# A two-layer decode block streaming 1.08 GB: chunk pairs in 32 KB rows at both ends of the stream, one memory for ring, weights and kept V, and V one slot further behind K

## The chip, the cores and the metric

The kernel runs on one core of one Trainium2 chip. The metric is the device time of one launch in microseconds (us), median of several runs. Engines are named as in the profile: PE (TensorE matmul), PEld (its weight load), DVE (VectorE), ACT (ScalarE), POOL (GpSimd) and SP (SyncE, which issues nearly all DMAs here).

## The reference, cut to what matters

```python
# x: (2, 1, 512); k_cache, v_cache: (2, 8, 32768, 128); wq: (512, 4096); wo: (4096, 512), all float32
x = x + A(layernorm(x))      # grouped-query attention over the cache
x = x + B(layernorm(x))      # token-mixing MLP, F = 1792
x = x + A(layernorm(x))      # the same caches and weights again
x = x + B(layernorm(x))
# A: q = x @ wq, 32 query heads, 4 of them share one of 8 K/V heads
#    p = softmax(q k^T / sqrt(128)); o = p v; return o @ wo
# B: y = w2 . gelu(w1 * layernorm(x) + b1) + b2, per channel
```

The caches of one layer are 537 MB and do not fit on the chip, so both layers read them from memory: about 1.08 GB in one launch.

## The kernel before, in words

The work is cut into 32 **units**: 2 layers x 2 batch rows x 8 K/V heads. A unit's K and its V are cut into 8 **chunks** each of 2 MB (128 partitions, rows of `CK` = 4096 floats, 16 KB). In main memory a chunk is one contiguous block, so a row of 16 KB is followed at once by the next partition's row.

One hand-written loop over **slots** `s` sets the whole order (lines 553 to 563): in slot `s` the kernel loads and uses K chunk `s` (counted over all units), then V chunk `s - 8 - LAG`. So V runs one unit and `LAG` = 1 slot behind K. Two tables, `pre` and `post`, hang the small steps onto slots: `make_q` (the query for the next unit, L171), `max_1`, `max_2` and the exponentials (L219 to L235), `denominators` (L300), `out_1` and `out_2` (L315 to L331), and the mixer of a finished layer row.

`k_chunk` (L183) takes a tile of the pool `ring`, issues the load on SP (L187), and runs 8 matmuls of 512 columns (L196; 16 in the trace, since a float32 matmul is two passes). `v_chunk` (L250) does the same for V (L265, matmuls L275). The pool has `RING` = 3 tiles of 2 MB, shared by K and V: a load can be issued once the matmuls on the chunk three loads earlier are done.

Weights lie in 16 tiles of 1 MB of their own (`wq_sb`, `wo_sb`), each loaded once during the first nine units. For the last head of a layer, part of V (`KEPT`: all of chunk 0, half of chunk 4) stays in the tile `kept` for the second layer, so a few loads are half size or fall away. The very last V chunk is loaded in four pieces (`PIECES`, 16, 8, 4 and 4 of its 32 column groups), so that its matmuls can begin early. After it comes `last_mixer` (L375 on), the closing mixer, whose scratch tiles are two ring tiles; its Gelu runs (L448) are cut where a run would cross from one tile to the other.

The units are ordered so that a layer's mixer runs while other units stream.

Of the kernel before, what the change touches and what calls it, by code (L numbers as in the profile page):

```python
# [8 lines left out]
F32 = mybir.dt.float32  # L9
AF = mybir.ActivationFunctionType  # L10
# [3 lines left out]
P = 128  # L14
CK = 4096
JT = CK // P
NG = 4
SUB = 2
PACK = 4
RING = 3  # L20
LAG = 1
KEPT = {0: 8, 4: 4}
BRIDGE = 3
PIECES = (16, 8, 4, 4)
THIN = 8
QT = 4
GELU_GROUPS = (2, 4, 4, 4)
# [6 lines left out]
def gqa_mixer_kernel(ctx: ExitStack, tc: tile.TileContext, x, kt, v, wq, wo, cols, out):  # L34
# [6 lines left out]

    nc = tc.nc
    B, D = x.shape
    U, NCH, DH, _ = kt.shape
    HKV = U // B
    R = wo.shape[2] // D
    DT = D // P
    FT = (cols.shape[1] - 1) // 3  # L50
    LAYERS = 2
    NU = LAYERS * U
# [3 lines left out]
    assert DH == P and R * PACK * SUB == 32 and PACK * SUB == 2 * QT and DT == NG and R == NG and D == 512  # L56

    const = ctx.enter_context(tc.tile_pool(name="const", bufs=1))
    ring = ctx.enter_context(tc.tile_pool(name="ring", bufs=RING))
    work = ctx.enter_context(tc.tile_pool(name="work", bufs=2))  # L60
    hidden = ctx.enter_context(tc.tile_pool(name="hidden", bufs=1))
    pscore = ctx.enter_context(tc.tile_pool(name="pscore", bufs=2, space=bass.MemoryType.PSUM))
# [6 lines left out]
    nc.vector.memset(xrow, 0.0)  # L69
    for b in range(B):  # L70
        nc.sync.dma_start(xrow[32 * b : 32 * b + 1, :], x[b : b + 1, :])
    wq_sb = [const.tile([P, DT, R * DH], F32, name=f"wq{h}") for h in range(HKV)]
    wo_sb = [const.tile([P, R, D], F32, name=f"wo{h}") for h in range(HKV)]

    def load_wq(h):
        nc.sync.dma_start(wq_sb[h].rearrange("p t c -> p (t c)"), wq[h])

    def load_wo(h):
        nc.sync.dma_start(wo_sb[h].rearrange("p t c -> p (t c)"), wo[h])

    load_wq(0)
    cols_sb = const.tile([P, 3 * FT + 1], F32, name="cols_sb")
# [76 lines left out]
    def unit_of(n):  # L159

        return units[n]
# [18 lines left out]

    sc_ps, S, mx, lsum, oT = {}, {}, {}, {}, {}

    def k_chunk(n, c):  # L183

        layer, b, h = unit_of(n)
        kc = ring.tile([P, CK], F32, name="chunk")
        nc.sync.dma_start(kc, kt[b * HKV + h, c])  # L187
        half, i = divmod(c, PACK)
        if i == 0:
            sc_ps[n] = pscore.tile([P, 512], F32, name="scores")  # L190
        w = CK // (NG * SUB)
        for k in range(SUB):
            at = R * (SUB * i + k)
            q = qpad[n % 2][:, 28 - at : 60 - at]
            for g in range(NG):
                nc.tensor.matmul(  # L196
                    sc_ps[n][32 * g : 32 * g + 32, :],
                    q,
                    kc[:, (k * NG + g) * w : (k * NG + g + 1) * w],
                    start=(i == 0 and k == 0),  # L200
                    stop=(i == PACK - 1 and k == SUB - 1),
                )
        if i == PACK - 1:
            if half == 0:
                S[n] = work.tile([P, HALVES, 512], F32, name="S")
                mx[n] = work.tile([P, HALVES, R], F32, name="mx")
            nc.vector.transpose(S[n][:, half, :], sc_ps[n])  # L207
            nc.vector.tensor_reduce(  # L208
                mx[n][:, half, :],
                S[n][:, half, :].rearrange("p (t h) -> p h t", h=R),  # L210
                axis=AX.X,
                op=ALU.max,
            )
# [27 lines left out]
                accum_out=lsum[n][:, h : h + 1],  # L241
            )

    kept = const.tile([P, sum(KEPT.values()) * QT * DH], F32, name="kept")
    place, at_kept = {}, 0
    for c, quads in KEPT.items():
        place[c] = at_kept
        at_kept += quads * QT * DH

    def v_chunk(n, c):  # L250
        layer, b, h = unit_of(n)
        u = b * HKV + h
        stay = KEPT.get(c, 0) if h == HKV - 1 else 0
        w = QT * DH
        very_last = n == NU - 1 and c == NCH - 1
        if stay:
            own = kept[:, place[c] : place[c] + stay * w]
            if layer == 0:
                nc.sync.dma_start(own, v[u, c, :, : stay * w])
        if stay < JT // QT:  # L260
            vc = ring.tile([P, CK], F32, name="chunk")
            f0 = stay * w
            for k in PIECES if very_last else (JT - stay * QT,):
                part = slice(f0, f0 + k * DH)
                nc.sync.dma_start(vc[:, part], v[u, c, :, part])  # L265
                f0 += k * DH
        half, i = divmod(c, PACK)


        a, c2 = divmod(i, PACK // 2)  # L270
        quads = JT // QT - (THIN // QT if very_last else 0)
        for q in range(quads):
            g = q % NG
            col = (c2 * (JT // QT) + q) * 32 + a * R * QT
            nc.tensor.matmul(  # L275
                acc[32 * g : 32 * g + R * QT, :],
                S[n][:, half, col : col + R * QT],
                (own if q < stay else vc)[:, q * w : (q + 1) * w],
                start=(c == 0 and q < NG),
                stop=(c == NCH - 1 and q >= quads - NG),  # L280
            )

        for j in range(quads * QT, JT):
            q, t = divmod(j, QT)
            g = j % NG
            col = (c2 * (JT // QT) + q) * 32 + a * R * QT + t * R
            nc.tensor.matmul(
                acc[32 * g : 32 * g + R, :DH],
                S[n][:, half, col : col + R],
                vc[:, j * DH : (j + 1) * DH],  # L290
                start=False,
                stop=True,
                skip_group_check=True,
            )
# [80 lines left out]
    def last_mixer(n):  # L375


        layer, b, h = unit_of(n)
        key = (layer, b)
        w = D // 2  # L380
        rw = rows[b]
        y = row_tile()
        p = px[key]
# [14 lines left out]
        for k in range(2):  # L398
            c = slice(k * w, (k + 1) * w)
# [4 lines left out]
        for g in range(NG):  # L404
            c = slice(g * P, (g + 1) * P)
# [4 lines left out]
        deviation(rs, mv)  # L410
        off = work.tile([P, 1], F32, name="off", bufs=1)
        nc.vector.tensor_scalar_mul(off, mv[:, 0:1], -1.0)
        space = [ring.tile([P, CK], F32, name="chunk") for _ in range(2)]
        tiles = [space[k // JT2][:, (k % JT2) * D : (k % JT2 + 1) * D] for k in range(2 * JT2)]
        flat = tiles[2 * JT2 - 1]
        nc.vector.tensor_copy(flat, p)
        scale = work.tile([P, FT], F32, name="scale", bufs=1)
        bias = work.tile([P, FT], F32, name="bias", bufs=1)
# [3 lines left out]
        def project(f):  # L422
            for g in range(NG):
                nc.tensor.matmul(  # L424
                    acc[32 * g : 32 * g + 1, :P],
                    w2c[:, f : f + 1],
                    tiles[f][:, g * P : (g + 1) * P],
                    start=False,
                    stop=(f == FT - 1),
                    skip_group_check=True,  # L430
                )
# [6 lines left out]
        f0 = DIRECT  # L438
        for m in TAIL_GROUPS:
            for f in range(f0, f0 + m):  # L440
                nc.vector.tensor_scalar(
                    tiles[f], flat, scale[:, f : f + 1], bias[:, f : f + 1], op0=ALU.mult, op1=ALU.add
                )

            cut = [f0] + [k for k in (JT2,) if f0 < k < f0 + m] + [f0 + m]
            for lo, hi in zip(cut, cut[1:]):
                u = space[lo // JT2][:, (lo % JT2) * D : ((hi - 1) % JT2 + 1) * D]
                nc.scalar.activation(u, u, AF.Gelu_apprx_tanh)  # L448
            for f in range(f0, f0 + m):
                project(f)  # L450
            f0 += m
        assert f0 == FT
        o = work.tile([P, P], F32, name="o", bufs=1)
# [3 lines left out]
                out[b : b + 1, g * P : (g + 1) * P], o[32 * g : 32 * g + 1, :]  # L457
            )

    JT2 = CK // D  # L460

    hid = {}

# [42 lines left out]
    pre, post = {}, {}  # L506
# [4 lines left out]
    for n in range(NU):  # L511
        layer, b, h = unit_of(n)
# [12 lines left out]
        at(pre, s0 + NCH + 2, denominators, n)  # L525
        e = s0 + 2 * NCH + LAG
        at(pre, e, out_1, n)
# [22 lines left out]
    for r in range(R):  # L550
        make_q(0, r)

    last = max(max(pre), max(post), NU * NCH + NCH + LAG - 1)
    for s in range(last + 1):
        if s < NU * NCH:
            k_chunk(*divmod(s, NCH))
        for f, a in pre.get(s, ()):
            f(*a)
        t = s - NCH - LAG
        if 0 <= t < NU * NCH:  # L560
            v_chunk(*divmod(t, NCH))
        for f, a in post.get(s, ()):
            f(*a)


def _layout(A_x, A_k_cache, A_v_cache, A_wq, A_wo, B_w1, B_b1, B_w2, B_b2):

    import numpy as np

    B, HKV, SK, DH = A_k_cache.shape  # L570
    D = A_x.shape[-1]
    n = SK // CK


    kt = A_k_cache.reshape(B * HKV, n // PACK, 2, PACK // 2, NG, 32, JT // QT, QT // SUB, SUB, DH)
    kt = kt.transpose(0, 1, 2, 7, 9, 8, 4, 3, 6, 5)
    wq = A_wq.reshape(D // P, P, HKV, -1).transpose(2, 1, 0, 3)
    wo = A_wo.reshape(HKV, -1, DH, D).transpose(0, 2, 1, 3)
    cols = [a.reshape(P, -1) for a in (B_w1, B_b1, B_w2)] + [np.broadcast_to(B_b2.reshape(1, 1), (P, 1))]
    return {  # L580
        "x": A_x.reshape(B, D),
        "kt": np.ascontiguousarray(kt).reshape(B * HKV, n, DH, CK),
        "v": A_v_cache.reshape(B * HKV, n, P, JT * DH),
        "wq": np.ascontiguousarray(wq).reshape(HKV, P, -1),
        "wo": np.ascontiguousarray(wo).reshape(HKV, DH, -1),
        "cols": np.concatenate(cols, axis=1),
    }
# [25 lines left out]
```

## Time and profile before

| | us |
|---|---|
| median of 3 runs | 2573.92 |
| lowest and highest of the 3 | 2573.39, 2575.07 |
| the profiled execution | 2575.11 |
| its span, first to last instruction | 2573.2 |
| outside the span | 1.9 |
| last V matmul ends | 2554.3 |

The profiled execution is 1.2 us above the median. Its span and the 1.9 us around it make up its own time. The granted TensorE clock was 0.782 of full speed on average.

### The profile page before, as it was taken

The page shows a single profiled execution, that of the slowest core. Times are in us where ns is not written, and L with a number is a line of the kernel's source. Part 1 is how long each engine was busy: PE and PEld are TensorE (multiplying, and loading weights), DVE is VectorE, ACT ScalarE, POOL GpSimd, SP SyncE. Part 2 cuts the span into 40 slices and gives each one's busy share as a digit, 9 for nine tenths or more (in the row PEclk, how much of TensorE's full clock was granted, in tenths as well). Part 3 has the DMA queues.
Part 4 walks back from the last instruction along what each step waited for, and adds up shares of the span by engine and source line. Part 5 has one row for each costly group of instructions (what it writes and reads, how often), then busy time and mean ns, then how long its engine had stood idle before and what let it go on. Part 6 is the DMA issues. An engine that isn't in the chain of part 4 may idle for free.

```text
span 2573.2 us, 22459 instructions
## 1 busy us (share of the span) xinstructions
PE 1678.5 (65%) x10208; PEld 490.2 (19%) x10208; DVE 215.0 (8%) x457; ACT 137.2 (5%) x287; POOL 4.8 (0%) x17
## 2 busy tenths in 40 slices
PE   7655656575766666666666666667667766666666
PEld 3111211121211112211211112212112212112112
DVE  1000000000011000000000000001100200000001
ACT  0000000000010000000000000001000100000001
POOL 0000000000000000000000000000000000000000
PEclk7777777777788878778777777788878887877877
DMA  9999999999999999999999999999999999999996
GB/s 398 429 427 427 427 427 425 428 426 427 425 427 426 427 423 423 428 427 428 427 425 427 427 427 426 428 423 427 428 425 428 422 427 428 427 426 427 426 427 274
DMA packets 76717, 1085.73 MB, mean 422 GB/s; under 512 B 8647, under 2 KB 8651, under 8 KB 9038
## 3 DMA queue, kind: packets, MB, share of 16 engines
q1 hardware_dynamic: 76472, 1084.27, 99.4%
q8 instruction: 80, 1.31, 0.2%
q14 instruction: 15, 0.12, 0.0%
q10 hardware_dynamic: 150, 0.03, 0.0%
HBM read 1084.25 MB, written 0.00 MB: 421 GB/s over the span
## 4 chain that ended last, share of the span: by engine, by line
DMA 76%; PE 23%; issue 1%; DVE 0%; ACT 0%; SPq 0%; POOL 0%; DVEq 0%; ACTq 0%; POOLq 0%
DMA chunk<-in_kt_dram 39%; DMA chunk<-in_v_dram 36%; PE scores L196 11%; PE acc L275 10%; PE misc L171 1%; PE misc L152 0%; PE misc L318 0%; PE rows L485 0%; ACT chunk L448 0%; ACT S L235 0%; ACT chunk L434 0%; PE rows L331 0%; PE misc L221 0%; PE acc L424 0%; DMA xrow<-in_x_dram 0%
## 5 line engine op out<-in xcount | busy, mean ns | idle before, releaser
L196 PE MATMUL scores<-chunk,qpad 128*32 128x512 f32 x4096 | 695.9, 813 | 467.9 <-DMA chunk<-in_kt_dram 467.2
L275 PE MATMUL acc<-chunk,S 128*16 128x512 f32 x3996 | 676.3, 809 | 408.6 <-DMA chunk<-in_v_dram 407.5
L196 PEld LDWEIGHTS scores<-chunk,qpad 128*32 128x32 f32 x4096 | 134.7, 130 | 903.7 <-DMA chunk<-in_kt_dram 463.8
L275 PEld LDWEIGHTS acc<-chunk,S 128*16 128x16 f32 x3996 | 108.8, 110 | 795.9 <-DMA chunk<-in_v_dram 531.4
L235 ACT ACTIVATE S<-S,neg 128x256 f32<-128x256 f32 x128 | 95.5, 751 | 2255.7 <-DVE neg L231 2255.7
L171 PEld LDWEIGHTS misc<-xnT,wq 128*128 128x128 f32 x1024 | 153.1, 230 | 157.1 <-issue 157.1
L171 PE MATMUL misc<-xnT,wq 128*128 128x1 f32 x1024 | 163.6, 282 | 0.0
L207 DVE STREAM_TRANSPOSE S<-scores 128x512 f32<-128x512 f32 x64 | 45.9, 717 | 626.5 <-PE scores L196 626.5
L179 DVE COPY qpad<-misc 128x4 f32<-128x4 f32 x32 | 5.2, 161 | 796.0 <-PE misc L171 796.0
L208 DVE TENSOR_REDUCE mx<-S 128x4 f32<-128x512 f32 x64 | 67.9, 1061 | 2.2
L318 PEld LDWEIGHTS misc<-selg,row 128*128 128x128 f32 x256 | 37.2, 224 | 39.7 <-issue 37.9
L318 PE MATMUL misc<-selg,row 128*128 128x4 f32 x256 | 40.0, 279 | 1.4 <-DVE row L315 0.9
L331 PE MATMUL rows<-wo,oT 128*1 128x512 f32 x248 | 37.3, 670 | 0.0
L223 DVE TENSOR_REDUCE m<-misc 4x1 f32<-4x128 f32 x32 | 8.9, 279 | 234.8 <-PE misc L221 234.8
L478 ACT ACTIVATE hid<-hid 128x2048 f32<-128x2048 f32 (+1 forms) x12 | 20.4, 1697 | 123.7 <-DVE hid L470 123.7
L302 DVE RECIPROCAL rl<-misc 128x4 f32<-128x4 f32 x32 | 5.8, 181 | 242.8 <-PE misc L300 242.8
L470 DVE TENSOR_SCALAR hid<-row,cols_sb 128x512 f32<-128x512 f32 x42 | 20.2, 542 | 57.4 <-PE rows L485 57.4
L235 ACT ACTIVATION_READ_ACCUMULATOR S<-S,neg 128x1 f32 x128 | 24.0, 188 | 0.0
L315 DVE COPY row<-acc 128x512 f32<-128x512 f32 x31 | 21.1, 680 | 0.0
L227 PEld LDWEIGHTS misc<-ident,m 4*128 4x128 f32 x64 | 11.8, 228 | 40.2 <-issue 39.5
L326 DVE TENSOR_TENSOR oT<-misc,rl 128x4 f32<-128x4 f32 x32 | 5.2, 161 | 157.4 <-PE misc L318 157.4
L300 PEld LDWEIGHTS misc<-lsum,one 128*128 128x128 f32 x64 | 10.8, 207 | 30.9 <-issue 30.9
(75 smaller groups left out, 199.0 us busy)
## 6 DMA issues: line engine op xcount, KB each, us to landing
chunk<-in_kt_dram SPq DMA_DIRECT2D x256, 2048.0 KB, 12.1
chunk<-in_v_dram SPq DMA_DIRECT2D x247, 2048.0 KB, 11.6
wq<-in_wq_dram SPq DMA_DIRECT2D x8, 1024.0 KB, 16.4
wo<-in_wo_dram SPq DMA_DIRECT2D x8, 1024.0 KB, 13.9
chunk<-in_v_dram SPq DMA_DIRECT2D x5, 1024.0 KB, 11.4
kept<-in_v_dram SPq DMA_DIRECT2D x2, 2048.0 KB, 17.7
kept<-in_v_dram SPq DMA_DIRECT2D x2, 1024.0 KB, 13.3
chunk<-in_v_dram SPq DMA_DIRECT2D x1, 512.0 KB, 10.2
```

The source lines that it names most:

```text
L171: nc.tensor.matmul(q_ps[n][:, r : r + 1], wq_sb[h][:, d, r * DH : (r + 1) * DH], xnT[layer, b][:, d : d + 1], start=(d == 0), stop=(d == D ...
L196: nc.tensor.matmul(sc_ps[n][32 * g : 32 * g + 32, :], q, kc[:, (k * NG + g) * w : (k * NG + g + 1) * w], start=(i == 0 and k == 0), stop=( ...
L207: nc.vector.transpose(S[n][:, half, :], sc_ps[n])
L208: nc.vector.tensor_reduce(mx[n][:, half, :], S[n][:, half, :].rearrange("p (t h) -> p h t", h=R), axis=AX.X, op=ALU.max,)
L227: nc.tensor.matmul(pm[:, :R], m4[n].to_broadcast([R, P]), ident[:R, :R], start=True, stop=True)
L235: nc.scalar.activation(s[:, :, h], s[:, :, h], AF.Exp, bias=neg[:, h : h + 1], scale=SCALE, accum_out=lsum[n][:, h : h + 1],)
L275: nc.tensor.matmul(acc[32 * g : 32 * g + R * QT, :], S[n][:, half, col : col + R * QT], (own if q < stay else vc)[:, q * w : (q + 1) * w], ...
L315: nc.vector.tensor_copy(asb, acc)
L318: nc.tensor.matmul(po[:, :R], asb[:, t * DH : (t + 1) * DH], selg[:, t * R : (t + 1) * R], start=(t == 0), stop=(t == QT - 1),)
L331: nc.tensor.matmul(rows[b][32 * r : 32 * r + 1, :], oT[n][:, r : r + 1], wo_sb[h][:, r, :], start=(units[n] == lay[layer, b][0]), stop=(un ...
L470: nc.vector.tensor_scalar(u[:, k * D : (k + 1) * D], hx[key], w1c[:, f : f + 1], b1c[:, f : f + 1], op0=ALU.mult, op1=ALU.add,)
L478: nc.scalar.activation(u[:, : n * D], u[:, : n * D], AF.Gelu_apprx_tanh)
```

## The change

In the slots 0 to 47 and from 212 on (`PAIRED`), two neighbouring chunks of K, or of V, are loaded by one DMA of 4 MB with rows of 32 KB, and used one after the other. In between, loads stay at 2 MB. The caches are laid out in main memory so that a row holds the pair (32 KB); a single chunk then reads 16 KB of each 32 KB row. `LAG` is 2, so that V pairs start on even slots.

Ring, kept V and weights move into one tile `mem`. In the first stretch a ring of three 4 MB buffers covers places whose weights and kept V are loaded later; in the last stretch it covers places whose weights and kept V have been used. In between, the ring is three 2 MB buffers in a fixed place. Within a paired slot the order is K load, both K chunks, the slot's `pre` steps, V load, both V chunks, `post`, then `pre` and `post` of the odd slot. The last V pair is loaded in five pieces: 32, 16, 8, 4 and 4 column groups. `last_mixer` has one scratch buffer of 4 MB, so no Gelu run is cut.

```diff
-LAG = 1
+PAIRED = ((0, 48), (212, 1 << 30))
+LAG = 2
-PIECES = (16, 8, 4, 4)
+PIECES = (32, 16, 8, 4, 4)
...
+    W = R * D
+    RING0 = W
+    KEPT0 = RING0 + RING * CK
+    kept_columns = sum(KEPT.values()) * QT * DH
+    order = [("q", 0), None, ("o", HKV - 1), ("q", HKV - 1), ("o", HKV - 2)]
+    order += [k for h in range(HKV) for k in (("q", h), ("o", h)) if k not in order]
...
+    mem = const.tile([P, f], F32, name="mem")
...
+    def places(base, k, size):
+        return [base + (j % RING) * size for j in range(k, k + RING)]
+
+    PLACES = (
+        (PAIRED[0][0], [], places(RING0, 0, 2 * CK)),
+        (PAIRED[0][1], [RING0 + j * CK for j in (2, 3, 4)], places(RING0, 0, CK)),
+        (PAIRED[1][0], [], [2 * 2 * CK, 0, 2 * CK]),
+    )
+    turn = {}
+
+    def buffer(s, size):
+        k = max(j for j in range(len(PLACES)) if PLACES[j][0] <= s)
+        _, ahead, loop = PLACES[k]
+        i = turn.get(k, 0)
+        turn[k] = i + 1
+        f = ahead[i] if i < len(ahead) else loop[(i - len(ahead)) % len(loop)]
+        return mem[:, f : f + size]
...
+    def load_k(s):
+        n, c = divmod(s, NCH)
+        layer, b, h = unit_of(n)
+        m = 2 if paired(s) else 1
+        t = buffer(s, m * CK)
+        f0 = (c % 2) * CK
+        nc.sync.dma_start(t, kt[b * HKV + h, c // 2, :, f0 : f0 + m * CK])
+        for j in range(m):
+            k_at[n, c + j] = t[:, j * CK : (j + 1) * CK]
...
-        kc = ring.tile([P, CK], F32, name="chunk")
-        nc.sync.dma_start(kc, kt[b * HKV + h, c])
+        kc = k_at.pop((n, c))
...
+    def load_v(s):
+        n, c = divmod(s - NCH - LAG, NCH)
...
+        t = buffer(s, m * CK)
+        k0 = stay * QT
+        for k in PIECES if s + m == NU * NCH + NCH + LAG else (m * JT - k0,):
+            nc.sync.dma_start(t[:, k0 * DH : (k0 + k) * DH], v[u, c // 2, :, f0 + k0 * DH : f0 + (k0 + k) * DH])
+            k0 += k
...
-        space = [ring.tile([P, CK], F32, name="chunk") for _ in range(2)]
+        space = buffer(NU * NCH, 2 * CK)
...
+    while s <= last:
+        m = 2 if paired(s) else 1
+        t = s - NCH - LAG
+        if s < NU * NCH:
+            load_k(s)
+            for j in range(m):
+                k_chunk(*divmod(s + j, NCH))
+        run(pre, s)
+        if 0 <= t < NU * NCH:
+            load_v(s)
+            for j in range(m):
+                v_chunk(*divmod(t + j, NCH))
+        run(post, s)
+        for j in range(1, m):
+            run(pre, s + j)
+            run(post, s + j)
+        s += m
...
-        "kt": np.ascontiguousarray(kt).reshape(B * HKV, n, DH, CK),
-        "v": A_v_cache.reshape(B * HKV, n, P, JT * DH),
+        "kt": np.ascontiguousarray(kt).reshape(B * HKV, n // 2, DH, 2 * CK),
+        "v": A_v_cache.reshape(B * HKV, n // 2, P, 2 * JT * DH),
```

More of the change, by code (lines that the diff above doesn't have):

```diff
@@ L45, in gqa_mixer_kernel @@
     B, D = x.shape
-    U, NCH, DH, _ = kt.shape
+    U, NCP, DH, _ = kt.shape
+    NCH = 2 * NCP
     HKV = U // B
@@ L58, in gqa_mixer_kernel @@
     const = ctx.enter_context(tc.tile_pool(name="const", bufs=1))
-    ring = ctx.enter_context(tc.tile_pool(name="ring", bufs=RING))
     work = ctx.enter_context(tc.tile_pool(name="work", bufs=2))
@@ L71, in gqa_mixer_kernel, with paired @@
         nc.sync.dma_start(xrow[32 * b : 32 * b + 1, :], x[b : b + 1, :])
-    wq_sb = [const.tile([P, DT, R * DH], F32, name=f"wq{h}") for h in range(HKV)]
-    wo_sb = [const.tile([P, R, D], F32, name=f"wo{h}") for h in range(HKV)]
+    W = R * D
[4 more added lines that the diff above has]
+    order += [k for h in range(HKV) for k in (("q", h), ("o", h)) if k not in order]
+    home, f = {}, 0
+    for k in order:
+        if k is None:
+            f = KEPT0 + kept_columns
+        else:
+            home[k] = f
+            f += W
+    mem = const.tile([P, f], F32, name="mem")
+    kept = mem[:, KEPT0 : KEPT0 + kept_columns]
+    wq_sb = [mem[:, home["q", h] : home["q", h] + W].rearrange("p (t c) -> p t c", t=DT) for h in range(HKV)]
+    wo_sb = [mem[:, home["o", h] : home["o", h] + W].rearrange("p (t c) -> p t c", t=R) for h in range(HKV)]
     def load_wq(h):
-        nc.sync.dma_start(wq_sb[h].rearrange("p t c -> p (t c)"), wq[h])
+        nc.sync.dma_start(mem[:, home["q", h] : home["q", h] + W], wq[h])
     def load_wo(h):
-        nc.sync.dma_start(wo_sb[h].rearrange("p t c -> p (t c)"), wo[h])
+        nc.sync.dma_start(mem[:, home["o", h] : home["o", h] + W], wo[h])
+    def places(base, k, size):
[13 more added lines that the diff above has]
+        return mem[:, f : f + size]
+    def paired(s):
+        return any(a <= s < b for a, b in PAIRED)
     load_wq(0)
@@ L181, in gqa_mixer_kernel @@
     sc_ps, S, mx, lsum, oT = {}, {}, {}, {}, {}
+    k_at, v_at = {}, {}
+    def load_k(s):
[7 more added lines that the diff above has]
+            k_at[n, c + j] = t[:, j * CK : (j + 1) * CK]
     def k_chunk(n, c):
-        layer, b, h = unit_of(n)
-        kc = ring.tile([P, CK], F32, name="chunk")
-        nc.sync.dma_start(kc, kt[b * HKV + h, c])
+        kc = k_at.pop((n, c))
         half, i = divmod(c, PACK)
@@ L242, in max_2 @@
             )
-    kept = const.tile([P, sum(KEPT.values()) * QT * DH], F32, name="kept")
     place, at_kept = {}, 0
@@ L248, in gqa_mixer_kernel, with stays, v_chunk @@
         at_kept += quads * QT * DH
-    def v_chunk(n, c):
+    def stays(n, c):
+        return KEPT.get(c, 0) if unit_of(n)[2] == HKV - 1 else 0
+    def load_v(s):
+        n, c = divmod(s - NCH - LAG, NCH)
         layer, b, h = unit_of(n)
         u = b * HKV + h
-        stay = KEPT.get(c, 0) if h == HKV - 1 else 0
+        m = 2 if paired(s) else 1
+        w = QT * DH
+        f0 = (c % 2) * CK
+        stay = stays(n, c)
+        if stay and layer == 0:
+            nc.sync.dma_start(kept[:, place[c] : place[c] + stay * w], v[u, c // 2, :, f0 : f0 + stay * w])
+        if stay == JT // QT:
+            return
+        t = buffer(s, m * CK)
[4 more added lines that the diff above has]
+        for j in range(m):
+            v_at[n, c + j] = t[:, j * CK : (j + 1) * CK]
+    def v_chunk(n, c):
         w = QT * DH
         very_last = n == NU - 1 and c == NCH - 1
+        stay = stays(n, c)
         if stay:
             own = kept[:, place[c] : place[c] + stay * w]
[L258 to L266, printed above, removed]
+        vc = v_at.pop((n, c), None)
         half, i = divmod(c, PACK)
@@ L412, in last_mixer @@
         nc.vector.tensor_scalar_mul(off, mv[:, 0:1], -1.0)
-        space = [ring.tile([P, CK], F32, name="chunk") for _ in range(2)]
-        tiles = [space[k // JT2][:, (k % JT2) * D : (k % JT2 + 1) * D] for k in range(2 * JT2)]
-        flat = tiles[2 * JT2 - 1]
+        space = buffer(NU * NCH, 2 * CK)
+        tiles = [space[:, k * D : (k + 1) * D] for k in range(JT2)]
+        flat = tiles[JT2 - 1]
         nc.vector.tensor_copy(flat, p)
@@ L443, in last_mixer @@
                 )
[L445 to L448, printed above, removed]
+            u = space[:, f0 * D : (f0 + m) * D]
+            nc.scalar.activation(u, u, AF.Gelu_apprx_tanh)
             for f in range(f0, f0 + m):
@@ L458, in last_mixer @@
             )
-    JT2 = CK // D
+    JT2 = 2 * CK // D
     hid = {}
@@ L551, in gqa_mixer_kernel, with run @@
         make_q(0, r)
+    def run(where, s):
+        for f, a in where.get(s, ()):
+            f(*a)
     last = max(max(pre), max(post), NU * NCH + NCH + LAG - 1)
-    for s in range(last + 1):
+    s = 0
+    while s <= last:
+        m = 2 if paired(s) else 1
+        t = s - NCH - LAG
         if s < NU * NCH:
[L556 to L559, printed above, removed]
+            load_k(s)
+            for j in range(m):
+                k_chunk(*divmod(s + j, NCH))
+        run(pre, s)
         if 0 <= t < NU * NCH:
-            v_chunk(*divmod(t, NCH))
-        for f, a in post.get(s, ()):
-            f(*a)
+            load_v(s)
+            for j in range(m):
+                v_chunk(*divmod(t + j, NCH))
[4 more added lines that the diff above has]
+        s += m
 def _layout(A_x, A_k_cache, A_v_cache, A_wq, A_wo, B_w1, B_b1, B_w2, B_b2):
@@ L572, in _layout @@
     n = SK // CK
-    kt = A_k_cache.reshape(B * HKV, n // PACK, 2, PACK // 2, NG, 32, JT // QT, QT // SUB, SUB, DH)
-    kt = kt.transpose(0, 1, 2, 7, 9, 8, 4, 3, 6, 5)
+    kt = A_k_cache.reshape(B * HKV, n // PACK, PACK // 2, NG, 32, 2, JT // QT, QT // SUB, SUB, DH)
+    kt = kt.transpose(0, 1, 2, 9, 7, 8, 3, 5, 6, 4)
     wq = A_wq.reshape(D // P, P, HKV, -1).transpose(2, 1, 0, 3)
```

## The prediction, made before the changed kernel had run

> **What bounds the kernel now.** I read the page's slices first, then its DMA part, then the windows by stretch, then the timeline of the end.
>
> ```profile
> PE   7655656575766666666666666667667766666666
> PEclk7777777777788878778777777788878887877877
> DMA  9999999999999999999999999999999999999996
> GB/s 398 429 427 427 427 427 425 428 426 427 425 427 426 427 423 423 428 427 428 427 425 427 427 427 426 428 423 427 428 425 428 422 427 428 427 426 427 426 427 274
> ...
> q1 hardware_dynamic: 76472, 1084.27, 99.4%
> ...
> DMA 76%; PE 23%; issue 1%; DVE 0%; ACT 0%; SPq 0%; POOL 0%; DVEq 0%; ACTq 0%; POOLq 0%
> ```
>
> The DMA row is full in every slice but the last, PE is about two thirds busy, and the rate sits between 422 and 429 GB/s for the whole run. The chain of waits gives PE 23%, but that is PE handing a buffer back while two other loads are queued; the queue's packets fill 99.4% of the 16 DMA engines' span. The windows say the same by stretch (columns: window, length, PE, PEld, DVE, ACT, POOL busy, granted clock, DMA share, GB/s):
>
> ```profile
> 64.00:480.00 416.00, 252.09 (x1530) 69.69 (x1534) 26.19 (x54) 15.45 (x40) 0.00 (x0) 0.77 1.01 427
> 480.00:2080.00 1600.00, 1055.80 (x6428) 305.14 (x6420) 141.82 (x297) 89.31 (x178) 2.75 (x5) 0.79 1.01 426
> 2080.00:2500.00 420.00, 276.99 (x1642) 78.24 (x1646) 26.28 (x55) 15.40 (x40) 0.00 (x0) 0.77 1.01 427
> ```
>
> A DMA share of 1.01 means that at no time is an engine without a packet (records overlap by a few ns). Counted over the packet records, all 16 engines together have under 2 us of idle time between the first packet at about 2.7 us and the last data at 2553.0 us. So the time is three parts: 2.7 us to start, 2550.3 us of an unbroken stream, 20.2 us of closing work after the last byte. Only what changes the work of the packets, or the two ends, can move it; waits inside the stream are worth nothing unless they empty the queue.
>
> So the packet is what to price. The trace holds size and duration of each; medians on the main queue, all of them busy-stream packets of one row each:
>
> ```
>     4 B (completion)     9 ns   x8500
>  2048 B                 84 ns   x258
>  4096 B                159 ns   x128
>  8192 B                312 ns   x2944   (fastest in twenty: 309)
> 16384 B                613 ns   x64640  (fastest in twenty: 611)
> ```
>
> From 2 to 4 KB a packet grows by 75 ns, from 4 to 8 KB by 150 to 153, from 8 to 16 KB by 301. That is 75 ns for each 2 KB, and 9 ns for each packet, whatever its size: 84 = 75 + 9, 159 = 150 + 9. The 4-byte packet shows the 9 ns alone.
>
> **The change, part by part.**
>
> *32 KB rows.* Bytes stay the same (`KEPT` is untouched, and the units with kept V lie outside `PAIRED`). A pair was two loads, 16 packets of 16 KB and 2 completions on each engine; it becomes 8 packets of 32 KB and 1 completion. No packet of 32 KB is in this trace. Continuing the ladder, it takes 613 + 2 x 302 = 1217 ns against 2 x 613 = 1226: it saves 9 ns. From below, if part of the fixed cost already overlaps (right after many a 4-byte packet the next one begins 5 ns later, not 9), it saves 5; from above, by the means of the 8 and 16 KB packets (316 and 617, disturbed ones included), 2 x 316 - 617 = 15. I take 9, the row nearest to it being the 4-byte packet. It could also cost, since nothing bounds it but the ladder; that is the second half of the slower rival. Per pair: 8 x 9 + 9 = 81 ns. Pairs: K in slots 0 to 46, 24, and 212 to 254, 22; V in slots 10 to 46, 19, and 212 to 262, 26; the last V pair is in pieces of 16 KB rows and less, as before, and gains nothing. 91 pairs x 81 ns = **7.4 us** (4.1 by 5 ns, 12.3 by 15 ns).
>
> The Trainium skill has a lower price for a packet: "DMA: Bandwidth & Descriptors", section "Why small descriptors are slow (HBM only)", gives about 3 cycles of fixed cost and 32 bytes of descriptor data. With the page's 850 MHz and 32-byte beats that is some 4.7 ns, an estimate, which would make 3.9 us of the 7.4. The 9 ns of the 4-byte packet speaks against it.
>
> *16 KB of a 32 KB row in the middle.* The single loads of slots 48 to 211 now skip 16 KB between rows. The nearest row: V half loads (1024 KB, 8 KB out of each 16 KB row) at 1690 and 2010 us have packets of 312 and 313 ns on the mean, contiguous weight loads 309 to 313. So a skip costs nothing there, and I take 0; if it costs, see the slower rival.
>
> *The queue must not run dry.* In a paired stretch there are three buffers of 4 MB, 9.7 us of stream each. A chunk takes PE 3.6 us at the low clock and 1.9 at the high one, so a pair is freed 7.3 us after landing at worst, plus three `make_q` in a row (3 x 1.87 us), while 19.4 us of loads lie queued. Before, it was 3.6 us against 9.8. That is cover enough for the bunching. At slot 212 the second pair needs the last two single chunks to be used (3.6 us after the second lands), and by then one 4 MB load is ahead of it. At the start, three pairs are queued without a wait; the first lands at about 17 us, and PE's first scores before began at 16.52, after `make_q`. Nothing is lost at either place. SP issues some 90 loads fewer, off the path.
>
> *LAG 2 and the order of steps.* K leads by one more slot, so the stream ends with 10 V chunks instead of 9; the bytes are the same. The moved steps (`max_2`, `out_1`, the mixers) use PE, DVE and ACT, which have a third or more to spare. Taken as 0; their cover is the queue of two loads.
>
> *The end.* Here PE does count:
>
> ```profile
> 2537.93 3.27 PE L275 MATMUL acc<-chunk,S 128*16 128x512 f32 x16 [2.99 <-DMA chunk<-in_v_dram]
> ...
> 2542.82 1.91 PE L275 MATMUL acc<-chunk,S 128*16 128x512 f32 x16 [1.62 <-DMA chunk<-in_v_dram]
> ...
> 2547.71 5.31 PE L275 MATMUL acc<-chunk,S 128*16 128x512 f32 x28 [2.98 <-DMA chunk<-in_v_dram]
> ```
>
> Before, each chunk is used as it lands, 4.9 us apart, so PE is idle when the pieces come. After, the last whole pair lands some 9.8 us ahead of the last piece, and PE then has four chunks to do: 4 x 1.91 = 7.6 us at the high clock, in time; 4 x 3.62 = 14.5 us at the low clock, so 4.7 us after the last piece, where before it was 0.4: 4.3 us late. The six chunks from 2525 to 2548 mostly ran at 1.91, so I take **+0.5 us** (0 to 4.3). The Gelu runs after it, five activations in 5.26 us (L448), become four: **-0.2 us** (0 to -0.5).
>
> *Sum.* -7.4 + 0.5 - 0.2 = -7.1 us. The profiled execution's own 2575.11 would become 2568.0 (span 2566.1); the median of the runs shown, 1.2 us below it, 2573.92 - 7.1 = **2566.8 us**.
>
> **The rivals.** What a measurement of this kernel can tell from no change is about 0.2%, 5.1 us: the line is 2568.8.
>
> *Half the fixed cost is already hidden* (0.12). At 5 ns a packet, 91 x (8 x 5 + 5) = 4.1 us; with the end's +0.3, 2570.1: the same. For it: the next packet's start 5 ns after a completion. Against it: growth by size leaves 9 ns at every step of the ladder. The skill's 3 cycles, above, would end here too.
>
> *Rows are cut into packets of 16 KB again* (0.08), that being the largest size in the trace. Only completions fall away: 91 x 9 ns = 0.8 us, 2573.4, the same. For it: even the code loads on queue q8 come in 16 KB. Against it: every K and V row was sent whole.
>
> *PE is late at the end* (0.06): -7.4 - 0.2 + 4.3 = -3.3, 2570.6, the same. For it: the 3.27 above; against it, its neighbours.
>
> *The new layout slows memory* (0.14). With rows 32 KB apart, engines that move in step read twice as far apart, in the paired loads and in the 64% of the stream that stays single. The slices already range from 429 to 422 GB/s; if the single stretch, about 1600 us (326 loads of 4.9 us), fell from 427 to 422, that is 1.2%, +19 us, and less the 7.1 it ends at 2586. It decides from a loss of 0.44% (7.1 of 1600), a 16 KB packet at 615.7 ns instead of 613. Against it: the half loads that skip. For it: the skill, same page, section "Latency and other measured facts", where copies slow down as the row pitch reaches large powers of two. The pitches that it lists begin at 512 KiB, far above 32; no run here shows one.
>
> **How the numbers follow.** The forecast has 0.60: faster, 2561 to 2568.8. "The same" has 0.12 + 0.08 + 0.06 = 0.26, slower 0.14. The range runs from the sum at 15 ns (2573.9 - 12.3 - 0.5 = 2561, less 1 for the spread of runs) to the rival of cut rows with part of the end's delay (2573.4 + 2.6): 2560 to 2576. What it leaves out is the slower rival and little else.
>
> **What the profile after would show.** Right: half the packets of the paired stretches at 32768 B and about 1217 ns; single-stretch packets still 613; GB/s about 430 in slices 2 to 7 and in the last seven, 427 between; no idle DMA; last data about 7 us earlier, closing work still 20 us. Wrong: packets of 16 KB only; 32 KB at 1226 or more; the middle below 426; or PE L275 busy without a gap into the closing copy (L307 before), with the tail longer than 20 us.

## The result and the profile after

| | before | after |
|---|---|---|
| median of 9 runs each | 2574.70 | 2566.88 |
| lowest and highest | 2573.20, 2576.35 | 2565.49, 2568.94 |
| profiled execution | 2575.11 | 2566.88 |
| its span | 2573.2 | 2565.1 |
| last byte of K or V, from the packet records | 2553.0 | 2544.0 |
| from there to the end of the span | 20.2 | 21.1 |

The change made the kernel faster: ratio 0.997, 95% interval 0.996 to 0.9981, which is 4.9 to 10.3 us with 7.8 between the medians. The smallest gain in that interval lies just under the 5.1 us at which the prediction drew its line between faster and the same. The forecast was 2566.8, 7.1 us below the 2573.92 known for before at the time.

From the page of the kernel after, the slices and the main queue (`...` marks lines left out):

```profile
DMA  9999999999999999999999999999999999999996
GB/s 409 432 429 430 432 429 430 423 428 425 427 428 425 423 428 425 427 428 427 426 427 424 427 428 427 423 427 428 425 426 427 424 431 432 433 430 430 431 432 267
...
q1 hardware_dynamic: 63368, 1084.26, 99.2%
```

The same megabytes go in 63368 packets instead of 76472. The rate steps up in just two places: slices 2 to 7 (429 to 432) and the last seven full ones (430 to 433). Between them it is what it was. The same by windows (length, then PE, PEld, DVE, ACT, POOL busy, granted clock, DMA share, GB/s):

```profile
64.00:480.00 416.00, 254.93 (x1554) 76.46 (x1549) 25.82 (x56) 18.10 (x48) 0.00 (x0) 0.76 1.00 430
480.00:2080.00 1600.00, 1061.29 (x6424) 301.02 (x6420) 143.85 (x297) 89.44 (x178) 2.75 (x5) 0.78 1.01 426
2080.00:2500.00 420.00, 264.55 (x1650) 82.47 (x1646) 27.47 (x58) 15.04 (x40) 0.00 (x0) 0.77 1.00 431
```

427, 426, 427 became 430, 426, 431. 3 in 427 over 416 us and 4 in 427 over 420 us are 2.9 + 3.9 = 6.8 us. The rates are whole numbers, so this is good to about 1 us only, and the paired packets do not fill the windows exactly (they run from 6 to 455 us and from 2063 to 2534). The DMA share stays at 1.00: the engines are as full as before and take less time for each byte.

The packet records hold exactly 11648 packets of 32768 B, 91 pairs x 128 rows, with a median of 1216 ns (1217 was forecast). The 16 KB packets that are left keep 613.

The two parts of the time moved apart: the last byte came 9.0 us earlier, the closing work took 0.9 us longer. Here is its beginning, first in the timeline of the kernel before, then in that of the kernel after:

```profile
2553.90 0.40 PE L287 MATMUL acc<-chunk,S 128*4 128x128 f32 x8 [0.66 <-DMA chunk<-in_v_dram]
2554.37 0.42 DVE L307 COPY row<-acc 128x256 f32<-128x256 f32 x1 [28.29 <-PE acc L287]
...
2557.82 0.70 PE L400 MATMUL bcast<-row,selg 128*128 128x256 f32 x2 [0.61 <-DVE row L307]
```

```profile
2543.14 1.04 PE L343 MATMUL acc<-mem,S 128*16 128x512 f32 x4 [0.20 <-DMA mem<-in_v_dram]
2543.78 0.33 PEld L355 LDWEIGHTS acc<-mem,S 128*4 128x4 f32 x8 [0.52 <-DMA mem<-in_v_dram]
2543.79 1.02 PE L355 MATMUL acc<-mem,S 128*4 128x128 f32 x16
2544.41 0.11 PEld L355 LDWEIGHTS acc<-mem,S 128*4 128x4 f32 x8 [0.31 <-DMA mem<-in_v_dram]
2544.88 0.42 DVE L375 COPY row<-acc 128x256 f32<-128x256 f32 x1 [28.72 <-PE acc L355]
...
2548.33 1.22 PE L468 MATMUL bcast<-row,selg 128*128 128x256 f32 x2 [0.62 <-DVE row L375]
```

The weight load ahead of the last V matmuls still waits for DMA (0.31 us), so PE was not late with the four chunks of the end: the closing copy starts 0.9 us after the last byte, against 1.4 before (2554.37 and 2553.0). What follows is slower: the L468 matmuls take 1.22 us where the same pair (L400 before) took 0.70. The windows of the last 22 us, before and then after, show a lower granted clock:

```profile
2551.20:2573.20 22.00, 12.60 (x184) 5.53 (x176) 8.82 (x23) 8.15 (x10) 0.55 (x1) 0.81 0.03 10
```

```profile
2543.10:2565.10 22.00, 13.96 (x176) 6.17 (x176) 8.83 (x23) 8.06 (x9) 0.55 (x1) 0.69 0.02 5
```

The granted clock of this stretch was 0.81 and is 0.69. Shorter windows show what these means are made of, before and then after:

```profile
2552.00:2562.20 10.20, 5.68 (x68) 2.63 (x62) 3.50 (x12) 0.91 (x3) 0.55 (x1) 1.00 0.01 4
2562.30:2569.00 6.70, 5.00 (x84) 2.20 (x88) 4.87 (x11) 6.70 (x8) 0.00 (x0) 0.50 0.01 2
```

```profile
2538.20:2548.30 10.10, 8.23 (x84) 2.49 (x76) 1.01 (x3) 0.39 (x1) 0.00 (x0) 1.00 0.32 127
2548.40:2561.90 13.50, 9.85 (x132) 4.38 (x132) 7.46 (x19) 7.59 (x8) 0.55 (x1) 0.50 0.01 2
```

The clock was full or half. The half stretch took 6.7 us of the closing work before and 13.5 after, and the slow L468 matmuls lie at its start. From the closing copy to the end of the span it took 18.9 us before and 20.2 after.

### The profile page after: what moved, and what is told of

It reads as the page before. It is cut to its first block, busy times and chain, and to the rows that moved or that the text cites. A ratio compares the mean times of both kernels' runs of the same rounds, so it can differ in the third digit from the quotient of the medians.

```text
span 2565.1 us, 22227 instructions
## 1 busy us (share of the span) xinstructions
PE 1665.0 (65%) x10208; PEld 494.2 (19%) x10208; DVE 215.3 (8%) x457; ACT 136.4 (5%) x286; POOL 4.8 (0%) x17
## 3 DMA queue, kind: packets, MB, share of 16 engines
q1 hardware_dynamic: 63368, 1084.26, 99.2%
## 4 chain that ended last, share of the span: by engine, by line
DMA 78%; PE 21%; issue 0%; DVE 0%; ACT 0%; SPq 0%; POOLq 0%; DVEq 0%; ACTq 0%
DMA mem<-in_kt_dram 40%; DMA mem<-in_v_dram 37%; PE acc L343 10%; PE scores L251 9%; PE misc L386 1%; PE misc L216 0%; PE acc L492 0%; PE misc L368 0%; DVE mx L263 0%; ACT S L290 0%; PE rows L550 0%; PE bcast L468 0%; DVE S L262 0%; DVE row L383 0%; PE rows L399 0%
## 5 line engine op out<-in xcount | busy, mean ns | idle before, releaser
L251 PE MATMUL scores<-mem,qpad 128*32 128x512 f32 x4096 | 692.5, 819 | 461.1 <-DMA mem<-in_kt_dram 461.0
L343 PE MATMUL acc<-mem,S 128*16 128x512 f32 x4092 | 694.2, 821 | 391.8 <-DMA mem<-in_v_dram 391.4
L251 PEld LDWEIGHTS scores<-mem,qpad 128*32 128x32 f32 x4096 | 145.1, 135 | 907.8 <-issue 471.6
L343 PEld LDWEIGHTS acc<-mem,S 128*16 128x16 f32 x4092 | 119.6, 115 | 837.6 <-DMA mem<-in_v_dram 529.5
L216 PEld LDWEIGHTS misc<-xnT,mem 128*128 128x128 f32 x1024 | 141.1, 216 | 119.4 <-issue 119.4
L216 PE MATMUL misc<-xnT,mem 128*128 128x1 f32 x1024 | 149.8, 271 | 0.0
L399 PE MATMUL rows<-mem,oT 128*1 128x512 f32 x248 | 36.7, 667 | 0.0
L535 DVE TENSOR_SCALAR hid<-row,cols_sb 128x512 f32<-128x512 f32 x42 | 20.2, 543 | 53.5 <-PE rows L550 53.4
L286 DVE TENSOR_SCALAR neg<-misc 128x4 f32<-128x4 f32 x32 | 5.2, 162 | 181.7 <-PE misc L282 181.7
L276 PE MATMUL misc<-ident,mxa 128*4 128x128 f32 x64 | 14.2, 308 | 7.5 <-DVE mxa L274 7.5
```

The lines of the kernel that those rows point to most:

```text
L216: nc.tensor.matmul(q_ps[n][:, r : r + 1], wq_sb[h][:, d, r * DH : (r + 1) * DH], xnT[layer, b][:, d : d + 1], start=(d == 0), stop=(d == D ...
L251: nc.tensor.matmul(sc_ps[n][32 * g : 32 * g + 32, :], q, kc[:, (k * NG + g) * w : (k * NG + g + 1) * w], start=(i == 0 and k == 0), stop=( ...
L276: nc.tensor.matmul(pm[:R, :P], mxa, ident, start=True, stop=True)
L343: nc.tensor.matmul(acc[32 * g : 32 * g + R * QT, :], S[n][:, half, col : col + R * QT], (own if q < stay else vc)[:, q * w : (q + 1) * w], ...
L399: nc.tensor.matmul(rows[b][32 * r : 32 * r + 1, :], oT[n][:, r : r + 1], wo_sb[h][:, r, :], start=(units[n] == lay[layer, b][0]), stop=(un ...
L535: nc.vector.tensor_scalar(u[:, k * D : (k + 1) * D], hx[key], w1c[:, f : f + 1], b1c[:, f : f + 1], op0=ALU.mult, op1=ALU.add,)
```

## The experiments

The theory: every DMA packet and every completion has a fixed cost of about 9 ns on its engine, and the change pays 91 x (8 + 1) fewer of them on each engine. Rivals: the deeper buffers, the extra slot of lag or the order of steps give the gain; fewer and larger loads give it, whatever their rows; the fixed cost is another size and something else makes up the rest. The first four variants are compared with 27 runs of before (median 2575.05), the next four with 21 others (median 2574.92).

**Layout and lag alone** (the kernel before, edited):

```diff
-LAG = 1
+LAG = 2
-nc.sync.dma_start(kc, kt[b * HKV + h, c])
+nc.sync.dma_start(kc, kt[b * HKV + h, c // 2, :, (c % 2) * CK : (c % 2) * CK + CK])
```

(V in the same way, and the layout of the changed kernel.)

> The kernel before with two parts of the change alone: the caches laid out in pairs (a single 2 MB load reads 16 KB of each 32 KB row) and V two slots behind K. No 4 MB loads, own tiles for ring, weights and kept V. Theory (the gain is the fixed cost of packets, so it comes with 32 KB rows alone): 0 +- 1.5 us against before, 16 KB packets at 613 ns. Rival one (the extra slot of lag or the order helps): 3 to 8 us faster. Rival two (skipping memory costs and the rows hide it): slower by 3 us or more, packets above 615 ns.

Measured: 2574.86 us, ratio 0.9997 (0.9988 to 1.0006). 16 KB packets: 613 ns, mean 616.9 as before. The two parts together make the time at most 3.1 us shorter or 1.5 us longer; reading 16 KB of each 32 KB row costs nothing that shows.

**The changed kernel with two loads for each pair:**

```diff
-nc.sync.dma_start(t, kt[b * HKV + h, c // 2, :, f0 : f0 + m * CK])
+for j in range(m):
+    nc.sync.dma_start(t[:, j * CK : (j + 1) * CK], kt[b * HKV + h, c // 2, :, f0 + j * CK : f0 + (j + 1) * CK])
```

> The changed kernel, but each 4 MB load is issued as two of 2 MB with rows of 16 KB into the same places; buffers of 4 MB, order, lag and memory stay. Theory (packets): the whole gain is gone, 0 to +1.5 us against before (the closing work of the changed kernel took 1 us more). Rival (three buffers of 4 MB keep the queue fuller, and that is the gain): still 6 to 8 us faster than before.

Measured: 2574.53 us, ratio 0.9994 (0.9986 to 1.0003), at most 3.6 us faster than before. The gain is gone: the slowest run of the changed kernel (2568.94) is faster than the fastest of this one (2572.26). Buffers, order, lag and memory are those of the changed kernel, so they do not carry it. Its windows are those of before, 427 and 428 where the changed kernel has 430 and 431:

```profile
64.00:480.00 416.00, 259.25 (x1535) 72.13 (x1534) 24.98 (x55) 18.49 (x48) 0.00 (x0) 0.75 1.01 427
2080.00:2500.00 420.00, 274.92 (x1638) 77.23 (x1630) 27.50 (x58) 15.36 (x40) 0.00 (x0) 0.76 1.01 428
```

**One 4 MB load of 16 KB rows** (the old layout, so that the rows of two chunks do not join):

```diff
-nc.sync.dma_start(t, kt[b * HKV + h, c // 2, :, f0 : f0 + m * CK])
+nc.sync.dma_start(t.rearrange("p (c f) -> p c f", c=m), kt[b * HKV + h, c : c + m].rearrange("c p f -> p c f"))
```

> The changed kernel with the old layout in main memory: a paired load is still one DMA of 4 MB, but of 16 packets of 16 KB on each engine (rows of two chunks that do not join). Only the second completion of each pair falls away. Theory (each packet has 9 ns or more of fixed cost): 91 x 9 ns = 0.8 us faster than before, at most 1.5, less up to 1 us of slower closing work. Rival (it is fewer and larger loads that pay, by fewer completions and issues): 6 to 8 us faster than before.

Measured: 2573.42 us, ratio 0.9990 (0.9981 to 0.9999). The page lines of this kernel, queue and sizes of loads:

```profile
q1 hardware_dynamic: 75016, 1084.26, 99.3%
...
mem<-in_kt_dram SPq DMA_DIRECT2D x46, 4096.0 KB, 23.1
mem<-in_v_dram SPq DMA_DIRECT2D x45, 4096.0 KB, 23.7
```

The loads are as few and as large as in the changed kernel, but there are only 1456 packets less than before, the completions (91 x 16). It gains 1.6 us by the medians, with an interval that runs from almost nothing to 4.9; 0.8 was expected. So large loads are not the main cause, and the share of the completions, 0.8 us by the theory, is not resolved. From here to the changed kernel only the rows differ, and the layout that makes them: 2573.42 to 2566.88 is 6.5 us for 91 x 8 = 728 packets less on each engine, 9.0 ns each. (The two were measured beside different runs of before, whose medians are 0.35 us apart; with each taken against its own, it is 6.2 us, 8.5 ns each.)

**Rows of 8 KB in every whole load** (the kernel before, caches laid out in half chunks):

```diff
-nc.sync.dma_start(kc, kt[b * HKV + h, c])
+nc.sync.dma_start(kc.rearrange("p (k f) -> p k f", k=2), kt[b * HKV + h, c].rearrange("k p f -> p k f"))
```

> The kernel before with rows of 8 KB in every 2 MB load: still 503 such loads, each now with 16 packets of 8 KB on every engine instead of 8 of 16 KB. This sizes the fixed cost on the other side, 8 more packets in each of 503 loads. At 9 ns a packet (the ladder of medians): 36 us slower than before, about 2610. At 12.7 ns (what a 32 KB packet saved in the changed kernel's stream): 51 us slower. At 5 ns (half of it hidden): 20 us slower. If size does not matter: 0.

Measured: 2611.8 us, ratio 1.0135 (1.0122 to 1.0149), against 2610 by the ladder. Queue and window of this kernel:

```profile
q1 hardware_dynamic: 141112, 1084.27, 99.9%
```

```profile
2080.00:2500.00 420.00, 272.24 (x1640) 78.70 (x1636) 26.60 (x57) 16.71 (x44) 0.00 (x0) 0.78 1.01 421
```

The queue has 141112 - 76472 = 64640 packets more, 4040 on each engine (the 503 chunks, and two whole chunks that go to `kept` and that the expectation did not count). The difference of the medians, 36.75 us, over 4040 is 9.1 ns a packet; the ratio gives 8.6, and its interval 7.8 to 9.5. Both 5 ns and 12.7 ns lie outside. This is the run that sizes the cost, since its effect is five times that of the change.

**Pairs in the first stretch alone, and in the last alone:**

```diff
-PAIRED = ((0, 48), (212, 1 << 30))
+PAIRED = ((0, 48), (1 << 29, 1 << 30))     # first alone; PIECES = (16, 8, 4, 4)
+PAIRED = ((0, 0), (212, 1 << 30))          # last alone
```

> The changed kernel with 4 MB loads and 32 KB rows in slots 0 to 47 alone (24 K pairs and 19 V pairs); from slot 48 on all loads are 2 MB of 16 KB rows, in the new layout and with V two slots behind. Theory (9 ns for each packet and completion saved, 8 + 1 per pair): 43 x 81 ns = 3.5 us faster than before, with up to 1 us given back in the closing work: 2.5 to 3.5. The rate is 430 in the window 64 to 480 us and 426 to 428 in 2080 to 2500. Rival (the gain comes from the last stretch, where V alone streams and PE is close behind): 0.

> The changed kernel with 4 MB loads and 32 KB rows from slot 212 on alone (22 K pairs and 26 V pairs). Theory: 48 x 81 ns = 3.9 us faster than before, up to 1 us given back in the closing work: 2.9 to 3.9; the rate is 426 to 428 in the window 64 to 480 us and 431 in 2080 to 2500. Rival (the gain comes from the last stretch alone): 7 to 8 us faster.

Measured: the first alone 2570.36 us, ratio 0.9982 (0.9973 to 0.9991), 2.3 to 7.0 us faster; the last alone 2569.16 us, ratio 0.9979 (0.9970 to 0.9988), 3.1 to 7.7. The theory's 3.5 and 3.9 lie in the intervals, but the medians are above it, 4.6 and 5.8, and add up to 10.3 where both together gave 7.8. So these two show where the gain is, not its size to the microsecond. Where it is stands in the windows, first alone and then last alone:

```profile
64.00:480.00 416.00, 253.78 (x1554) 76.44 (x1549) 25.82 (x56) 18.07 (x48) 0.00 (x0) 0.76 1.00 430
2080.00:2500.00 420.00, 268.84 (x1634) 73.12 (x1638) 28.65 (x58) 15.33 (x40) 0.00 (x0) 0.79 1.01 427
```

```profile
64.00:480.00 416.00, 259.02 (x1530) 71.83 (x1534) 25.98 (x53) 15.31 (x40) 0.00 (x0) 0.76 1.01 427
2080.00:2500.00 420.00, 274.70 (x1650) 82.71 (x1646) 27.47 (x58) 15.03 (x40) 0.00 (x0) 0.75 1.00 431
```

Each stretch has the higher rate only while it is paired. A gain from the last stretch alone, the rival's story, would leave the first at 0.

**The clock at the end: two and three slots of lag in the kernel before.**

```diff
-LAG = 1
+LAG = 2     # and, in the other run, 3
```

> The kernel before with V two slots behind K and nothing else, for one look at the closing work. The changed kernel and three variants, all two slots behind, had a granted clock of 0.69 in the last 22 us and about 1 us more closing work; before and the 8 KB variant, one slot behind, had 0.81. If the lag sets where the clock's ups and downs fall at the end: 0.69 again and 21 to 21.5 us from the last data to the end. If it is chance, or comes from the layout or the 4 MB buffers: 0.81 and 20.2 us. The time otherwise as before, 2573 to 2577.

> As the run with two slots of lag, with three. If the lag sets the clock at the end, a value of its own, and not that of one slot by rule; if chance, 0.69 or 0.81 without order. The stream is as before (rate 426 to 427, last data at 2552 to 2555 us): a lag of one more slot costs and gains nothing there.

Measured, one run each: 2575.82 and 2579.4 us. Windows of the last 22 us with two slots of lag, and of the last-stretch variant above, which has two as well:

```profile
2552.00:2574.00 22.00, 13.01 (x180) 5.94 (x174) 8.83 (x23) 8.15 (x10) 0.55 (x1) 0.81 0.01 2
```

```profile
2545.10:2567.10 22.00, 13.27 (x192) 5.61 (x184) 8.82 (x23) 8.06 (x9) 0.55 (x1) 0.83 0.05 17
```

Both have two slots of lag and a clock above 0.8, so the lag alone does not set it; nor do the 32 KB rows of the last stretch. Over ten profiled executions this window's clock was either about 0.69 (five) or 0.81 to 0.83 (five). What decides between them stayed open. The clock goes with the time from the closing copy to the end of the span: 19.9 to 20.5 us in the five at 0.69, 18.8 to 19.4 in the five others. What comes ahead of the copy is another matter. In the run with two slots the work after the last byte took 22.0 us at 0.81, neither 20.2 nor 21 to 21.5 as expected, because there PE was late: the copy came 2.5 us after the last byte (2554.59 and 2552.06), and PE had half the clock from 2543.3 to 2553.4 us:

```profile
2543.30:2553.40 10.10, 8.19 (x42) 1.33 (x36) 0.00 (x0) 0.00 (x0) 0.00 (x0) 0.50 0.69 279
```

The 8 KB variant shows the same: half the clock from 2579.7 to 2589.7 us, last byte at 2588.4, copy 2.5 us behind it. In the other eight executions the copy came 0.9 to 1.4 us after the last byte.

The run with three slots missed its expectation: the last byte came at 2557.7 us, not 2552 to 2555, and the window 900 to 1600 us ran at 424 GB/s. Counted over its packet records, an engine stood idle for 3.6 us of that window on average, against 0.4 in the profile of before, so the queue ran short there; what emptied it is not shown. It is a single run, 1.8 us above the highest of the 21 of before beside it but only 0.2 above the highest of the 27 (2579.2), so a cost of the third slot is not shown either.

## Why the prediction was right, point by point

*The stream.* The step that carried the forecast was 91 pairs x (8 packets + 1 completion) x 9 ns = 7.4 us. Its counts hold (11648 packets of 32 KB, 1456 completions less), and so does the price of a packet on either side of 16 KB: 9.1 ns by the medians with 8 KB rows everywhere, 8.5 to 9.0 between the two 4 MB variants. The 9 ns of a completion were not measured apart. The changed kernel is 7.7 us below its twin with two loads for each pair (7.3 with each taken against its own runs of before).

*Luck in the number.* The forecast of 2566.8 and the median of 2566.88 agree more closely than the working could. The forecast started from a median of 2573.92; over nine runs before has 2574.70. The gain was 7.8 where 7.1 was forecast, and the profiled execution came out at 2566.88 where 2568.0 was forecast.

*The bounds of that step.* The lower one, 5 ns, from packets that overlap, lies outside the interval of the 8 KB run, 7.8 to 9.5, and with it the first rival. So does the estimate of 4.7 ns that the prediction worked out from the Trainium skill's page "DMA: Bandwidth & Descriptors", section "Why small descriptors are slow (HBM only)". The upper one, 15 ns, came from the means of packet records. After the change they would still say so (2 x 616.9 - 1218.1 = 15.7 ns), while the time says 9. The medians (2 x 613 - 1216 = 10) and the ladder were the better reading.

*The profiled execution.* Its last byte came 9.0 us earlier, 1.6 more than the step. Four executions whose stream has no 32 KB packets (layout and lag, two loads, short rows, two slots of lag) put it at 2554.4, 2550.4, 2551.5 and 2552.1, and the one with three slots at 2557.7. Against such a spread between single executions, no cause can be shown for those 1.6.

*Taken as nothing, and nothing that shows:* the layout with two slots of lag (0.9997), and these with the deeper buffers and the bunched steps (0.9994, at most 3.6 us faster). The queue did not run dry in the paired stretches: by the packet records at least 16 packets were under way at every moment from 64 to 450 and from 2080 to 2530 us. The last rival, slower memory, needed 16 KB packets of 615.7 ns; their median stayed at 613 in every run with the new layout. The rival of cut rows is refuted by the packet sizes.

*The end.* This step came out wrong, though it is small. I took +0.5 us for PE being late with four chunks; it was on time, and the closing copy began 0.4 us sooner after the last byte. It had the full clock for its last chunks (1.00 from 2538.2 us on); the low clock, for which the step allowed 4.3 us, did not last through the closing chunks in any of the four profiles of kernels that end with a paired slot, so that bound stays untested. The Gelu runs, five in 5.26 us, became four in 5.16 (L513), 0.1 instead of 0.2. What the step left out is the granted clock of the closing work, 0.69 against 0.81 in these two profiles; from the closing copy on it took 1.3 us more. Since both values occur in kernels with and without pairs, this is not shown to be an effect of the change.

*Loose readings.* The 422 to 429 GB/s "for the whole run" leave out the first slice (398) and the last (274). And after most completions the next packet starts 6 ns later, not 5 (6620 and 1036 of the 8500). The sum rests on neither.

## What to carry to other kernels

When the DMA engines are never idle, price the packet, not the load: plot the median packet time against row size in the trace, and the intercept (the time left at size zero) is what each packet less saves. Here 9 ns on each packet made 8, 16 and 32 KB rows worth 421, 427 and 430 to 431 GB/s, while the size of the load, the depth of the buffers and the order of the steps gave at most a small part of the gain. To size such a small cost, make it larger (halve the rows everywhere) rather than measure its removal.

## What was not expected of the hardware

Differences between the means of packet records (15.7 ns) overstate what the time shows (9 ns). Records overlap (the DMA share was 1.01 of the time before and 1.00 after), but that this explains the whole of the difference is not shown. And the mean granted clock of the last 22 us fell on one of two values, 0.69 or about 0.82, in kernels whose closing work is the same but for a Gelu run, depending on how long a stretch of half clock (13.5 or 6.7 us in the two profiles above) fell into it; that moves single profiles by about 1 us at the end.
